# Float16 parts for every fourth group's value products in an attention and feed-forward kernel

## The chip, the cores and the metric

The kernel runs on one core of a Trainium2 chip. The metric is device time in microseconds (us), the median of three runs. The engines are TensorE (PE in the profile; PEld are its weight loads), VectorE (DVE), ScalarE (ACT), GpSimd (POOL) and SyncE (SP), which here issues nearly all DMAs.

## The reference

A transformer block in float32 with a sequence of 2048 rows, width 512, 32 heads of 16 and a hidden width of 1792:

```python
q, k, v = split(layernorm(x) @ wqkv)            # 32 heads of 16
p = softmax(q @ k.T * 16 ** -0.5)               # 2048 x 2048 for each head
h = x + concat(p @ v) @ wo
out = h + silu(layernorm(h) @ w1) @ w2          # w1 512 x 1792, w2 1792 x 512
```

## The kernel before

**Precision.** Most products are made as three float16 products: an operand x is written as a high part (x rounded to float16) and a rest (x minus that, in float16), and high x high, rest x high and high x rest are added in PSUM. `low` (a subtraction on DVE or POOL) makes the rest. The value products, weights p times v, are the exception: they are plain float32 products.

**Stages.** First come the layer norm, the projections and the measuring of the scales of the weights (powers of two). Queries and keys go to DRAM as parts (`qd`, `kd`) and come back for each item: an item is four heads with 512 queries, and there are 32 of them. Rows 0 to 47 of a head's tile hold three parts of 16 rows, and rows 48 to 63 of the query tile are fixed rows: two hold the negative of each query's largest score, the others are zero (`fix_q`). The key tile has a constant (`fix_k`, 2 ** 15) there. One product of 64 rows thus gives the score less its maximum, and the exponential follows without another pass.

**Groups and steps.** An item has 16 groups, a group is 128 keys of its four heads, and 512 steps walk through the groups. Step g makes the score products (`scores`, TensorE), their exponentials (ACT, into `pt` tiles), some searches for maxima of a later item (`maximum`: a product of 48 rows on TensorE and a reduction on DVE), and, at its end, the value products of group g - 2 (`values`, `LAG` is 2). The value products of four heads lie on four strips of 32 columns and add into one PSUM bank, `pv`, over the 16 groups of an item. At the end of an item the bank is copied (`pvs`, on ACT from item 8 on), and the sums and rows go by DMA through DRAM: `sums`, `invert` (POOL) and `spread` follow 2, 6 and 8 steps later, and `divide` (POOL) 10 steps later for every second item.

**The feed-forward part beside attention.** After every 8 items the 512 finished rows go through the output projection (items 8, 16 and 24) and then the feed-forward part. Its products run beside the groups from step 148, 276 and 404 on, 112 steps each: 56 steps of first products (w1) and 56 of second products (w2). There TensorE works on two halves of 64 rows at a time. `beside_products` writes that order by hand: an even step takes the scores of heads 0 and 2 of groups g and g + 1, the odd step after it those of heads 1 and 3 of both, four maxima come in each step, and six half products of the feed-forward part lie beside them. Three PSUM banks are left for scores and three for maxima. A first product ends with a scaling on ACT (`g`), a tanh two steps later and four operations on POOL; a second product takes 14 steps and ends with a scaling on ACT (`g`) and an addition on POOL one step later.

**Order.** Each engine runs its instructions in the order in which the program issues them; helpers pin it. In the profile, lines 99 (products), 102 (transposes), 106 (POOL), 113 (ACT), 123 (DVE) and 129 (DMAs on SP) are those helpers, and 305 and 307 the reductions for maxima.

**Rings.** Keys and queries of an item lie in one of five tiles (`RING`). The weights of the feed-forward part come through eight tiles (`raw_tile`), `pt` has 14 tiles, and `oh` in `zp` two.

Of the kernel before, what the change touches and what calls it, by code (L numbers as in the profile page):

```python
# [10 lines left out]
F32 = mybir.dt.float32  # L11
# [27 lines left out]
LN = 2.0 ** 10  # L39

BOUND = 23.0
PIECES = 14, 14, 4
# [5 lines left out]

LAG = 2
PTS = 14  # L50

RING = 5

HEADS = [(0, 1), (0, 0), (1, 1), (1, 0)]
# [37 lines left out]
def attention_mlp_kernel(ctx: ExitStack, tc: tile.TileContext, x, wqkv, wo, w1, w2, out):  # L92
# [100 lines left out]
    nc.gpsimd.memset(minus, -1.0)  # L193
    ones = const.tile([P, P], F32, name="ones")
    nc.gpsimd.memset(ones, 1.0)
    powers = const.tile([P, 4], F32, name="powers")
    both_s, both_w = powers[:, :2], powers[:, 2:]
    qk_s, qk_w, v_w = (powers[:, n:n + 1] for n in (0, 2, 3))
    qk_e, qk_0, v_f = (const.tile([P, 1], F32, name=name) for name in ("qk_e", "qk_0", "v_f"))

    factors = const.tile([P, 15], F32, name="factors")
    sigma, inverse = factors[:, :4], factors[:, 4:8]
    w1_s, w2_s, wo_s, o_s = (sigma[:, n:n + 1] for n in range(4))
# [47 lines left out]
    va = vpool.tile([P, KC, H, DH + 1], F32, name="va")  # L251

    def rows_of_head(t, h):
        return t[h * DH:(h + 1) * DH].rearrange("d s n -> (d s) n")

    def load_k(i, k, lo=0, n=S):
        a, j = HEADS[k]
        h = 4 * (i % 8) + 2 * a + j
        dma(ks[i % RING][64 * j:64 * j + 48, a, lo:lo + n], rows_of_head(kd, h)[:, lo:lo + n])

    def load_q(i, k):
        a, j = HEADS[k]
        h = 4 * (i % 8) + 2 * a + j
        lo = i // 8 * 512
        dma(qs[i % RING][64 * j:64 * j + 48, a, :], rows_of_head(qd, h)[:, lo:lo + 512])

# [24 lines left out]
    def maximum(i, kb, qt, a, j, n):  # L291

        piece = piece_of(i, a)
        width = 1 if i == LAST else 2
        if piece not in mx:
            mx[piece] = small.tile([P, 64], F32, name="mx", bufs=RING + 1)[:, :32 * width].rearrange(
                "p (j a q k) -> p j a q k", j=2, a=width, k=4)
            left[piece] = 32 * width
        heads = (0, 1) if j is None else (j,)
        for m, h in enumerate(heads):  # L300
            mm(space[:, n + m, :], qs[i % RING][64 * h:64 * h + 48, a, qt * P:qt * P + P],
               ks[i % RING][64 * h:64 * h + 48, a, kb * 512:kb * 512 + 512], start=True, stop=True)
        of = mx[piece][:, :, a % width, qt, kb]
        if j is None:
            pin(nc.vector.tensor_reduce(of, space[:, n:n + 2, :], axis=AX.X, op=ALU.max))  # L305
        else:
            pin(nc.vector.tensor_reduce(of[:, j:j + 1], space[:, n, :], axis=AX.X, op=ALU.max))  # L307
# [42 lines left out]
    def place_far(piece):  # L350

        i, a = piece
        n = 16 if a is None else 8
        mt = small.tile([P, P], F16, name="mt", bufs=1)
        pin(nc.sync.dma_start(mt, wide.pop(piece), transpose=True))
        split.pop(piece)

        def out():
            for j in range(2):
                rows = qs[i % RING][64 * j + 48:64 * j + 50, slice(None) if a is None else slice(a, a + 1)]  # L360
                dma(rows.rearrange("r a n -> r (a n)").rearrange("r (a b) -> r a b", b=P), mt[n * j:n * j + n, :])
            placed.add(piece)

        if at["attention"]:
            soon(1, out)
        else:
            out()

    def place_max(piece):

        i, a = piece
        ns = split.pop(piece)
        n = ns.shape[1]
        ps = bank("sm", F16)
        tr(ps[:n, :P], ns, ident_h)
        mt = small.tile([32, P], F16, name="mn", bufs=1)[:n]
        dve("tensor_copy", mt, ps[:n, :P])

        def out():
            for j in range(2):  # L380
                dst = qs[i % RING][64 * j + 48:64 * j + 50, slice(None) if a is None else slice(a, a + 1)]
# [108 lines left out]


    def pt_tile(name):
        return bp.tile([P, 512], F32, tag="pt", name=name, bufs=PTS)

    def scores(g, k, kind="st"):

        i = g // KC
        a, j, c = head(g, k)
        assert piece_of(i, a) in placed
        ps = bank(kind)  # L500
        mm(ps, ks[i % RING][64 * j:64 * j + 64, a, c * P:(c + 1) * P], qs[i % RING][64 * j:64 * j + 64, a, :],
           start=True, stop=True)
# [39 lines left out]

    rest_sq = const.tile([P, sum(PIECES)], F32, name="rest_sq")
    norms = const.tile([P, 4], F32, name="norms")
# [24 lines left out]
    def set_factors():  # L569
# [4 lines left out]
        for to, a, f in ((h_f, inverse[:, :1], 1 / LN), (g_s, w1_s, 1 / 32.0), (g_half, w1_s, 1 / 64.0),  # L574
                         (out_f, inverse[:, :1], 32.0), (o_minus, o_s, -1.0), (o_twice, o_s, 2.0)):
            pool("tensor_scalar", to, a, f, None, op0=ALU.mult)
        pool("tensor_tensor", out_f, out_f, inverse[:, 1:2], ALU.mult)
        pool("tensor_tensor", wo_f, inverse[:, 2:3], inverse[:, 3:], ALU.mult)
# [27 lines left out]
    def measure(meanwhile):  # L606
# [58 lines left out]
    def project_v(b, t):  # L665
# [3 lines left out]
              {k: (lambda n=n: burst(n)) for k, n in BESIDE_V1.get((b, t), {}).items()})  # L669
        act("mul", va[:, 4 * b + t, :, 0:DH], ps.rearrange("p (h d) -> p h d", d=DH), v_f)  # L670

# [99 lines left out]
    for b in range(NB):  # L771
# [7 lines left out]
        for n, (kind, k) in enumerate(units + vs if b else units):  # L779
# [160 lines left out]
    def finish_part():  # L940
        pvs = bp.tile([P, 512], F32, name="pvs", bufs=1)
        dve("tensor_copy", pvs, pv)
        o_t = zp.tile([P, 4, P], F32, name="o_t", tag="oh")
        pool("memset", o_t, 0.0)
# [4 lines left out]
    def divide_part(part, pvs, o_t, kind="st"):  # L949
# [3 lines left out]
        halves = ps.rearrange("p t (m j r) -> p t m j r", m=2, r=32)[:, :, :, :, :DH + 1]  # L953
        both = gp.tile([P, 4, 2, DH + 1], F32, name="both", bufs=1)
# [110 lines left out]
    def load_rows(b, t):  # L1065
        n = 4 * b + t
        if b < NB - 1:
            hx[t] = raw_tile()
        else:
            hx[t] = ks[(LAST + 1) % RING].rearrange("p a n -> p (a n)").bitcast(F32)[:, t * D:(t + 1) * D]  # L1070
        dma(hx[t], x[n * P:(n + 1) * P, :])
# [89 lines left out]
    def end_first(f, ps):  # L1161
# [3 lines left out]
        def bend():  # L1165
            t = zp.tile([P, 512], F32, name="t", tag="oh")
            act("activation", t, z, AF.Tanh, scale=0.5)
# [262 lines left out]
    def maxima(g):  # L1430

        i, c = divmod(g, KC)
        ready = at["ready"] = min(ITEMS, i + RING - (0 if c == KC - 1 else 1)) * 64
        late_now = at["step"] in late
# [26 lines left out]
    for g in range(groups):  # L1461
# [5 lines left out]
        if (g in beside) != (g - 1 in beside):  # L1467
# [37 lines left out]
        if g == 1:  # L1505
            dve("memset", pv, 0.0)
        at["group"] = g
        n = maxima(g)
# [75 lines left out]
```

## Time and profile before

| | |
|---|---|
| median of three runs | 1543.95 us (1543.88 to 1543.97) |
| the profiled execution | 1544.18 us, its span 1542.3 us |
| busy: TensorE, DVE, ACT, POOL | 1531.9, 1364.3, 1240.0, 575.1 us |
| granted TensorE clock | 1.0 |
| value products | 4096 records (two for each product), 539.1 us |

The profile is one execution. Busy time is the union of an engine's instructions. TensorE's instructions overlap as in a pipeline, so a product's own length (0.38 us for 512 columns of float16) is longer than the distance to the next start. A group's row gives the count, the busy time, the mean length in ns, and the idle time ahead of it with what ended it. In a timeline, rows are start, length, engine, line, operation, names, and a count where several of a kind follow each other.

### The profile page before, as it was taken

To read this page: it belongs to the slowest core of one execution; us is meant where nothing else is said; L and a number is where in the kernel's file an instruction comes from. 1 tells how busy PE (TensorE), PEld (TensorE's weight loads), DVE (VectorE), ACT (ScalarE), POOL (GpSimd) and SP (SyncE) were. 2 spreads that over 40 slices of the span, in tenths; PEclk is the share of its full clock that TensorE was granted. 3 is DMA by queue.
4 is the path that set the end of the run, shared out by engine and by line. 5 is a ranking of instruction groups with operands and counts; after the bars stand their busy time and mean duration, and the time that the engine had idled before them with its cause. 6 is when DMAs were issued, how large, how long until landed. Compare 5 with 4: busy or idle time off the path is not lost.

```text
span 1542.3 us, 30754 instructions
## 1 busy us (share of the span) xinstructions
PE 1531.9 (99%) x11408; PEld 494.6 (32%) x11408; DVE 1364.3 (88%) x2168; ACT 1240.0 (80%) x2410; POOL 575.1 (37%) x782
## 2 busy tenths in 40 slices
PE   9999999999999999999999999999999999999999
PEld 6433322222222333333322333333322333332354
DVE  7899999999999999999999999999999999994322
ACT  5555699999987899888888998888878889888632
POOL 6643453544544444411144444301153444212100
PEclk9999999999999999999999999999999999999999
DMA  6667423333434122245424112444433221335332
GB/s 220 167 170 237 135 80 93 119 96 109 111 89 103 35 63 63 82 147 152 144 64 103 43 46 62 123 131 129 140 81 92 57 56 43 103 103 168 111 91 74
DMA packets 137058, 163.32 MB, mean 106 GB/s; under 512 B 44112, under 2 KB 81040, under 8 KB 136908
## 3 DMA queue, kind: packets, MB, share of 16 engines
q1 hardware_dynamic: 132156, 152.85, 34.6%
q10 hardware_dynamic: 4752, 8.52, 2.1%
q8 instruction: 89, 1.46, 0.4%
q14 instruction: 61, 0.50, 0.1%
HBM read 126.48 MB, written 24.63 MB: 98 GB/s over the span
## 4 chain that ended last, share of the span: by engine, by line
PE 93%; DVE 3%; ACT 2%; issue 1%; POOL 0%; DMA 0%; SPq 0%; POOLq 0%; ACTq 0%
PE ps L99 93%; ACT pt L113 1%; DVE mx L305 1%; DVE mx L307 1%; PE ps L102 1%; DMA ks<-in_A_x_dram 0%; DVE pvs L123 0%; POOL wv_l L106 0%; DVE ks L123 0%; DVE st L123 0%; ACT pvs L113 0%; ACT g L113 0%; DVE ot L123 0%; DVE xtl L123 0%; POOL rs L106 0%
## 5 line engine op out<-in xcount | busy, mean ns | idle before, releaser
L307 DVE TENSOR_REDUCE mx<-ps 128x1 f32<-128x512 f32 x1842 | 1146.1, 682 | 56.2 <-PE ps L99 12.0
L113 ACT ACTIVATE pt<-ps 128x512 f32<-128x512 f32 x2048 | 1049.7, 606 | 130.8 <-PE ps L99 128.7
L99 PE MATMUL ps<-ks,qs 48*128 48x512 f16 x2048 | 666.9, 380 | 2.6 <-DVE mx L307 1.5
L99 PE MATMUL ps<-qs,ks 64*128 64x512 f16 x2048 | 624.8, 377 | 0.6
L99 PE MATMUL ps<-pt,va 128*17 128x512 f32 x4096 | 539.1, 598 | 0.6
L99 PE MATMUL ps<-hts,w 64*128 64x512 f16 (+2 forms) x1212 | 285.0, 372 | 0.0
L99 PEld LDWEIGHTS <-ks 64*128 64x128 f16 x2048 | 174.0, 94 | 223.8 <-issue 177.6
L99 PE MATMUL ps<-w,gates 64*128 64x512 f16 (+1 forms) x938 | 230.3, 378 | 0.2 <-ACT g L113 0.2
L99 PEld LDWEIGHTS <-qs 48*128 48x128 f16 x2048 | 166.4, 94 | 67.7 <-issue 28.4
L99 PEld LDWEIGHTS <-w 64*128 64x128 f16 (+1 forms) x1212 | 101.6, 95 | 236.9 <-ACT pt L113 107.2
L106 POOL TENSOR_TENSOR ri<-rc,minus 128x16 f32<-128x16 f32 x31 | 90.6, 2924 | 208.8 <-DMA rc<-dn 208.8
L99 PEld LDWEIGHTS <-gates 64*128 64x128 f16 (+1 forms) x1082 | 88.7, 95 | 222.5 <-ACT pt L113 97.8
L99 PEld LDWEIGHTS ps<-pt,va 128*17 128x17 f32 x4096 | 68.1, 95 | 195.3 <-issue 186.6
L305 DVE TENSOR_REDUCE mx<-ps 128x2 f32<-128x1024 f32 x103 | 119.1, 1218 | 4.3 <-PE ps L99 3.5
L113 ACT ACTIVATE g<-ps,factors 128x512 f32<-128x512 f32 x80 | 54.7, 684 | 65.1 <-PE ps L99 61.0
L106 POOL TENSOR_SCALAR t<-t,factors 128x512 f32<-128x512 f32 x42 | 29.0, 691 | 184.0 <-ACT t L113 184.0
L113 ACT ACTIVATE ks<-ps 128x512 f32<-128x512 f32 x30 | 17.9, 597 | 51.9 <-PE ps L99 46.6
L106 POOL TENSOR_TENSOR ot<-ot,g 128x512 f32<-128x512 f32 x12 | 15.3, 1271 | 111.6 <-ACT g L113 111.6
L123 DVE SCALAR_TENSOR_TENSOR gh<-g,factors,gh 128x512 f16<-128x512 f32 x14 | 10.5, 752 | 52.1 <-ACT gh L113 52.1
L106 POOL TENSOR_TENSOR t<-t,g 128x512 f32<-128x512 f32 x42 | 53.7, 1279 | 3.5
L106 POOL TENSOR_TENSOR sl<-ks,sh 128x512 f16<-128x512 f32 x30 | 34.7, 1156 | 50.4 <-ACT sh L113 36.9
L106 POOL TENSOR_SCALAR nm<-nm 128x16 f32<-128x16 f32 (+1 forms) x42 | 10.8, 256 | 107.1 <-DVE nm L321 105.5
(158 smaller groups left out, 1029.7 us busy)
## 6 DMA issues: line engine op xcount, KB each, us to landing
w<-w2d SPq DMA_DIRECT2D x182, 256.0 KB
ks<-kd SPq DMA_DIRECT2D x120, 192.0 KB
w<-w1d SPq DMA_DIRECT2D x56, 256.0 KB
ks<-in_B_w_dram ACTq DMA_DIRECT2D x28, 256.0 KB
w<-in_B_w_dram SPq DMA_DIRECT2D x28, 256.0 KB
qs<-qd SPq DMA_DIRECT2D x128, 48.0 KB
kd<-sh SPq DMA_DIRECT2D x16, 256.0 KB
qd<-sh SPq DMA_DIRECT2D x16, 256.0 KB
```

The lines of the kernel that those rows point to most:

```text
L99: return tc.keep_in_program_order(nc.tensor.matmul(*a, **k))
L102: tc.keep_in_program_order(nc.tensor.transpose(*a))
L106: tc.keep_in_program_order(getattr(nc.gpsimd, op)(*a, **k))
L113: ins = getattr(nc.scalar, fn)(*a, **k)
L123: pin(getattr(nc.vector, fn)(*a, **k))
L305: pin(nc.vector.tensor_reduce(of, space[:, n:n + 2, :], axis=AX.X, op=ALU.max))
L307: pin(nc.vector.tensor_reduce(of[:, j:j + 1], space[:, n, :], axis=AX.X, op=ALU.max))
```

## The change

For items 10 to 30, the value products of groups 1, 5, 9 and 13 of an item are made in float16 parts where the group and its neighbours lie beside second products (`in_halves`).
- The exponentials of such a group go to a float32 tile `raw` (from `oh`, now three tiles). The high part is copied to float16 on POOL for heads 0 and 1 and on ACT for heads 2 and 3; the rest is made on POOL. Both lie in the `pt` tile.
- `values` makes twelve float16 products for it: high x high for four heads, high weights x rest of v, rest of weights x high v.
- The parts of v for these four groups of keys are made once, in item 10, on POOL (`split_chunk`). They lie in the fifth tiles of the ring of keys and queries; from item 10 on the ring has four places (`slot`, `loaded`), so an item is loaded three items ahead instead of four. The maxima tiles `mx` go from six to four.
- The fixed rows of the queries hold a constant instead of zeros, made from the scale of queries and keys (`raised`): it raises all weighted scores by 2 ** 14, which drops out in the division by their sum.
- v is kept at another scale: `v_f` and the factor `o_s` go, and the first four chunks of `va` are multiplied by `v_s` on POOL. `ones` and `rest_sq` move to another pool of tiles, `both` to `oh`.

```diff
+RAISE = 14
+MOST = 2.0 ** 15
+HALVED = 1, 5, 9, 13
+FEWER = 2 * RING
...
-    nc.gpsimd.memset(fix_q, 0.0)
+    nc.gpsimd.memset(fix_q, 1.0)
+    raised = const.tile([16, 1], F32, name="raised")
...
+    def slot(i):
+        return i % RING if i < FEWER else (i - FEWER) % (RING - 1)
+    def loaded(i):
+        return min(ITEMS, i + RING if i < FEWER else max(FEWER + RING - 1, i + RING - 1))
...
+    def in_halves(g):
+        i, c = divmod(g, KC)
+        return FEWER <= i < LAST and c in HALVED and all((x - marks[0]) % (8 * KC) in range(BEHIND + 4 * FC, BEHIND + 8 * FC) for x in (g - 1, g + 3))
+    def split_chunk(n):
+        (h, l), v = split_v[n], va[:, HALVED[n]].rearrange("p h d -> p (h d)")
+        pool("tensor_copy", h, v)
+        low(l, v, h, "pool")
...
         def weigh():
             pts[g, k] = pt_tile("pt")
+            if in_halves(g):
+                raw, (h, l) = zp.tile([P, 512], F32, name="raw", tag="oh", bufs=3), halves_of(pts[g, k])
+                ins = act("activation", raw, ps, AF.Exp, scale=qk_f)
+                if k < 2:
+                    pool("tensor_copy", h, raw)
+                else:
+                    act("copy", h, raw)
+                low(l, raw, h, "pool")
+                return ins
             return act("activation", pts[g, k], ps, AF.Exp, scale=qk_f)
...
-        dve("reciprocal", v_f, v_w)
-        pool("tensor_scalar", v_f, v_f, 1 / LN, None, op0=ALU.mult)
...
+        pool("tensor_scalar", raised, qk_s[:16], qk_s[:16], RAISE * math.log(2) / (14 * MX * SCALE), op0=ALU.mult, op1=ALU.mult)
+        pool("tensor_scalar", raised, raised, MOST, None, op0=ALU.min)
+        pool("tensor_scalar", fix_q, fix_q, raised, 1.0, op0=ALU.mult, op1=ALU.mult)
...
+            if b == 2 and 2 <= n:
+                pool("tensor_scalar", va[:, n - 2, :, 0:DH], va[:, n - 2, :, 0:DH], v_s, 1.0, op0=ALU.mult, op1=ALU.mult)
...
     def values(g):
+        if in_halves(g):
+            h_l, v_l = [halves_of(pts.pop((g, k))) for k in range(4)], split_v[HALVED.index(c)]
+            for m, (x, v) in enumerate(((0, 0), (0, 1), (1, 0))):
+                for k in range(4):
+                    a, j, keys = head(g, k)
+                    h = 4 * (i % 8) + 2 * a + j
+                    mm(pv[32 * k:32 * k + DH + 1, :], v_l[v][:, (DH + 1) * h:(DH + 1) * (h + 1)], h_l[k][x],
+                       start=False, stop=m == 2 and c == KC - 1)
+            return
...
-        dve("tensor_scalar", rc, rc, o_s, None, op0=ALU.mult)
...
-        if i + RING - 1 < ITEMS and 6 <= c < 14:
-            (load_k if c % 2 else load_q)(i + RING - 1, c // 2 - 3)
+        if loaded(i) > loaded(i - 1) and 6 <= c < 14:
+            (load_k if c % 2 else load_q)(loaded(i) - 1, c // 2 - 3)
...
+        if i == FEWER and c % 3 == 2 and c < 12:
+            split_chunk(c // 3)
```

More of the change, by code (lines that the diff above doesn't have):

```diff
@@ L193, in attention_mlp_kernel @@
     nc.gpsimd.memset(minus, -1.0)
[L194 to L195 removed]
     powers = const.tile([P, 4], F32, name="powers")
[L197 removed]
+    both_s, both_w, v_s = powers[:, :2], powers[:, 2:], powers[:, 1:2]
     qk_s, qk_w, v_w = (powers[:, n:n + 1] for n in (0, 2, 3))
[L199 removed]
+    qk_e, qk_0 = (const.tile([P, 1], F32, name=name) for name in ("qk_e", "qk_0"))
     factors = const.tile([P, 15], F32, name="factors")
     sigma, inverse = factors[:, :4], factors[:, 4:8]
[L203 removed]
+    w1_s, w2_s, wo_s = (sigma[:, n:n + 1] for n in range(3))
     h_f, g_s, out_f, wo_f, o_minus, o_twice, g_half = (factors[:, n:n + 1] for n in range(8, 15))
     fix_q = const.tile([16, 512], F16, name="fix_q")
[L207 removed]
+    nc.gpsimd.memset(fix_q, 1.0)
+    raised = const.tile([16, 1], F32, name="raised")
     fix_k = const.tile([16, 512], F16, name="fix_k")
@@ L258, in load_k @@
         h = 4 * (i % 8) + 2 * a + j
[L259 removed]
+        dma(ks[slot(i)][64 * j:64 * j + 48, a, lo:lo + n], rows_of_head(kd, h)[:, lo:lo + n])
     def load_q(i, k):
@@ L264, in load_q @@
         lo = i // 8 * 512
-        dma(qs[i % RING][64 * j:64 * j + 48, a, :], rows_of_head(qd, h)[:, lo:lo + 512])
+        dma(qs[slot(i)][64 * j:64 * j + 48, a, :], rows_of_head(qd, h)[:, lo:lo + 512])
     def fixed_rows(i):
@@ L295, in maximum @@
         if piece not in mx:
-            mx[piece] = small.tile([P, 64], F32, name="mx", bufs=RING + 1)[:, :32 * width].rearrange(
+            mx[piece] = small.tile([P, 64], F32, name="mx", bufs=RING - 1)[:, :32 * width].rearrange(
                 "p (j a q k) -> p j a q k", j=2, a=width, k=4)
@@ L300, in maximum @@
         for m, h in enumerate(heads):
-            mm(space[:, n + m, :], qs[i % RING][64 * h:64 * h + 48, a, qt * P:qt * P + P],
-               ks[i % RING][64 * h:64 * h + 48, a, kb * 512:kb * 512 + 512], start=True, stop=True)
+            mm(space[:, n + m, :], qs[slot(i)][64 * h:64 * h + 48, a, qt * P:qt * P + P],
+               ks[slot(i)][64 * h:64 * h + 48, a, kb * 512:kb * 512 + 512], start=True, stop=True)
         of = mx[piece][:, :, a % width, qt, kb]
@@ L359, in out @@
             for j in range(2):
-                rows = qs[i % RING][64 * j + 48:64 * j + 50, slice(None) if a is None else slice(a, a + 1)]
+                rows = qs[slot(i)][64 * j + 48:64 * j + 50, slice(None) if a is None else slice(a, a + 1)]
                 dma(rows.rearrange("r a n -> r (a n)").rearrange("r (a b) -> r a b", b=P), mt[n * j:n * j + n, :])
@@ L380, in out @@
             for j in range(2):
-                dst = qs[i % RING][64 * j + 48:64 * j + 50, slice(None) if a is None else slice(a, a + 1)]
+                dst = qs[slot(i)][64 * j + 48:64 * j + 50, slice(None) if a is None else slice(a, a + 1)]
                 dst = dst.rearrange("r a n -> r (a n)").rearrange("r (a b) -> r a b", b=P)
@@ L489, in attention_mlp_kernel, with halves_of @@
     free = [sum(x not in fixed for x in range(g)) for g in range(groups + 1)]
+    def halves_of(t):
+        return t.bitcast(F16)[:, :512], t.bitcast(F16)[:, 512:]
+    width = H * (DH + 1)
+    spare_k, spare_q = (t.rearrange("p a n -> p (a n)") for t in (ks[RING - 1], qs[RING - 1]))
+    parts = [spare_k[:, n * width:(n + 1) * width] for n in range(7)] + [spare_q[:, :width]]
+    split_v = [(parts[n], parts[4 + n]) for n in range(4)]
     def pt_tile(name):
         return bp.tile([P, 512], F32, tag="pt", name=name, bufs=PTS)
+    def in_halves(g):
[5 more added lines that the diff above has]
+        low(l, v, h, "pool")
     def scores(g, k, kind="st"):
@@ L541, in attention_mlp_kernel @@
     sq = small.tile([P, 3], F32, name="sq", bufs=1)
-    rest_sq = const.tile([P, sum(PIECES)], F32, name="rest_sq")
+    rest_sq = wp.tile([P, sum(PIECES)], F32, name="rest_sq")
+    ones = wp.tile([P, P], F32, name="ones")
+    nc.gpsimd.memset(ones, 1.0)
     norms = const.tile([P, 4], F32, name="norms")
@@ L942, in finish_part @@
         dve("tensor_copy", pvs, pv)
-        o_t = zp.tile([P, 4, P], F32, name="o_t", tag="oh")
+        o_t = zp.tile([P, 4, P], F32, name="o_t", tag="oh", bufs=3)
         pool("memset", o_t, 0.0)
@@ L1165, in bend @@
         def bend():
-            t = zp.tile([P, 512], F32, name="t", tag="oh")
+            t = zp.tile([P, 512], F32, name="t", tag="oh", bufs=3)
             act("activation", t, z, AF.Tanh, scale=0.5)
@@ L1432, in maxima @@
         i, c = divmod(g, KC)
-        ready = at["ready"] = min(ITEMS, i + RING - (0 if c == KC - 1 else 1)) * 64
+        ready = at["ready"] = loaded(i if c == KC - 1 else i - 1) * 64
         late_now = at["step"] in late
```

12 lines of the change are left out of this document (7 added, 5 removed).

## The prediction

> **What bounds the kernel now.** First I read the page: the busy times, the chain that ended last, the costliest groups.
>
> ```profile
> span 1542.3 us, 30754 instructions
> ...
> PE 1531.9 (99%) x11408; PEld 494.6 (32%) x11408; DVE 1364.3 (88%) x2168; ACT 1240.0 (80%) x2410; POOL 575.1 (37%) x782
> ...
> PE ps L99 93%; ACT pt L113 1%; DVE mx L305 1%; DVE mx L307 1%; PE ps L102 1%; DMA ks<-in_A_x_dram 0%; DVE pvs L123 0%; POOL wv_l L106 0%; DVE ks L123 0%; DVE st L123 0%; ACT pvs L113 0%; ACT g L113 0%; DVE ot L123 0%; DVE xtl L123 0%; POOL rs L106 0%
> ...
> L99 PE MATMUL ps<-pt,va 128*17 128x512 f32 x4096 | 539.1, 598 | 0.6
> ```
>
> TensorE is the bound: 99% busy, 93% of the chain. The value products are 4096 records, two for each float32 product, so 512 groups of four heads. Next, the stretches that the change touches: busy time by engine (PE, PEld, DVE, ACT, POOL) in the second products, and the chain in the first of them.
>
> ```profile
> 641.00:770.00 129.00, 129.00 (x1088) 41.76 (x1088) 122.99 (x202) 105.69 (x205) 20.56 (x28) 1.00 0.47 142
> 976.00:1109.00 133.00, 133.00 (x1124) 43.02 (x1122) 126.84 (x208) 109.25 (x211) 24.00 (x34) 1.00 0.46 135
> 1317.00:1380.00 63.00, 63.00 (x534) 20.39 (x529) 60.14 (x100) 52.09 (x102) 10.31 (x17) 1.00 0.32 98
> ...
> 640.97 129.21 PE ps L99 x1085
> ```
>
> TensorE has no gap here, its clock is 1.00, and the chain is TensorE alone. ACT has 18% idle, POOL 84%, DVE 5%. A shorter value product is thus worth its whole saving, as long as ACT and DVE keep up.
>
> **The gain.** One step of that stretch, in order of time on TensorE (start, length):
>
> ```profile
> 700.03 0.39 PE L99 MATMUL ps<-w,gates 64*128 64x512 f16 x1
> ...
> 701.12 0.38 PE L99 MATMUL ps<-w,gates 64*128 64x512 f16 x1
> ...
> 701.33 0.38 PE L99 MATMUL ps<-ks,qs 48*128 48x512 f16 x1
> 701.35 0.37 PE L99 MATMUL ps<-qs,ks 64*128 64x512 f16 x1
> 701.65 0.62 PE L99 MATMUL ps<-pt,va 128*17 128x512 f32 x4
> ...
> 702.10 0.61 PE L99 MATMUL ps<-pt,va 128*17 128x512 f32 x4
> ...
> 702.64 0.39 PE L99 MATMUL ps<-w,gates 64*128 64x512 f16 x1
> 702.87 0.38 PE L99 MATMUL ps<-w,gates 64*128 64x512 f16 x1
> ```
>
> A step lasts 2.61 us (700.03 to 702.64). The four heads' products run side by side on four column strips: the first halves start at 701.65, the second at 702.10, the next product of another shape at 702.64: 0.45 + 0.54 = 0.99 us. A float16 product of 512 columns takes 0.21 us to the next start (701.12 to 701.33), 0.23 just after a change of shape (702.64 to 702.87); a float32 half is two such passes. Three rounds of float16: 0.23 + 0.23 + (0.54 - 0.21) = 0.79, so 0.20 us is saved in each split group. How four float16 strips follow each other no row shows; the bounds are 0.09 us more per round, if the third round's weights aren't loaded ahead, and 0.78 for the three at the plain spacing. I take 0.20.
>
> The condition in `in_halves` asks for items 10 to 30, every fourth group (1, 5, 9, 13 of 16), and neighbours in the second products, which are groups 204 to 259, 332 to 387 and 460 on. That leaves 205 to 253, 333 to 381 and 461 to 493: 13 + 13 + 9 = 35 groups. 35 x 0.20 = **7.0 us gained**.
>
> **What ACT pays.** Of a split group, heads 0 and 2 get their exponentials at the end of the even step, 1 and 3 at the end of the odd one. The last of each (2 and 3) is followed on ACT by a copy to float16. Rows of ACT: a step with nothing added, one with the copy of the value sums (`pvs`), one with a product's scaling (`g`), and the nearest row to the new copy.
>
> ```profile
> 690.25 2.06 ACT L113 ACTIVATE pt<-ps 128x512 f32<-128x512 f32 x4 [0.55 <-PE ps L99]
> 692.32 0.58 ACT L113 COPY pvs<-ps 128x512 f32<-128x512 f32 x1
> 692.84 0.60 ACT L113 ACTIVATE pt<-ps 128x512 f32<-128x512 f32 x1
> ...
> 669.32 1.10 ACT L113 ACTIVATE pt<-ps 128x512 f32<-128x512 f32 x2 [0.54 <-PE ps L99]
> 670.31 0.68 ACT L113 ACTIVATE g<-ps,factors 128x512 f32<-128x512 f32 x1
> 670.88 2.14 ACT L113 ACTIVATE pt<-ps 128x512 f32<-128x512 f32 x4
> ...
> 175.50 0.60 ACT L113 ACTIVATE ks<-ps 128x512 f32<-128x512 f32 x1 [0.17 <-PE ps L99]
> 176.13 0.62 ACT L113 CAST sh<-ks 128x512 f16<-128x512 f32 x1
> 176.65 0.59 ACT L113 ACTIVATE pt<-ps 128x512 f32<-128x512 f32 x1
> ```
>
> Four exponentials take 2.06 us, and ACT then idles 0.55 us for the next step's first score. A copy of what ACT has just written starts 0.03 us after the write's end (175.50 + 0.60, 176.13) and holds the next instruction up by 0.52 (176.13 to 176.65): 0.55 in all. It just fits the gap. The `pvs` copy alone (0.52) and `g` alone (0.57) fit it too. Two of them don't: ACT is then about 0.52 to 0.57 us late. What lateness costs is shown by four rows of another stretch, where ACT's first exponential of a step came late:
>
> ```profile
> 832.17 2.06 ACT L113 ACTIVATE pt<-ps 128x512 f32<-128x512 f32 x4 [0.58 <-PE ps L99]
> ...
> 832.77 0.38 PE L99 MATMUL ps<-ks,qs 48*128 48x512 f16 x1
> 832.82 0.37 PE L99 MATMUL ps<-qs,ks 64*128 64x512 f16 x1
> 833.12 1.05 PE L99 MATMUL ps<-pt,va 128*17 128x512 f32 x8
> ...
> 700.67 1.59 ACT L113 ACTIVATE pt<-ps 128x512 f32<-128x512 f32 x3 [0.54 <-PE ps L99]
> ```
>
> Three score banks are left in these steps, so the fourth score waits for the first exponential: it starts 0.05 us after that one's end (832.17 + 0.60, 832.82), and the value products stand behind it. In a normal step the first exponential ends at 701.27 and the fourth score starts at 701.35: 0.08, so 0.03 us of slack. A late ACT thus costs TensorE its lateness less 0.03, once; the shifted step then gives ACT its gap back.
> - Copies in a step with nothing else: lateness 0.00 to 0.03, cost 0 each; if the cover is gone, 70 x 0.01 and up (a rival below).
> - Group 1 of an item: its odd step also has the `pvs` copy of the item before. These are 209, 225, 241, 337, 353, 369, 465, 481: 8 x (0.52 - 0.03) = **3.9 us lost**.
> - A second product ends every 14 steps, at 217, 231, 245, 345, 359, 373, 473, 487; 217, 245, 345, 373 and 473 are split steps, where `g` meets the copy: 5 x (0.57 - 0.03) = **2.7 us lost**.
>
> **What POOL pays.** Two copies and four subtractions per split group; nearest rows, then what already runs there.
>
> ```profile
> L106 POOL TENSOR_TENSOR gates<-t,gates 128x512 f16<-128x512 f32 x42 | 48.6, 1158 | 3.4
> ...
> L106 POOL CAST gates<-t 128x512 f16<-128x512 f32 x42 | 25.6, 610 | 2.7
> ...
> 700.01 2.92 POOL L106 TENSOR_TENSOR ri<-rc,minus 128x16 f32<-128x16 f32 x1 [21.93 <-DMA rc<-dn]
> ...
> 703.78 0.22 POOL L106 TENSOR_TENSOR ri<-ri,rc 128x16 f32<-128x16 f32 x1
> 707.65 1.27 POOL L106 TENSOR_TENSOR ot<-ot,g 128x512 f32<-128x512 f32 x1 [3.65 <-ACT g L113]
> ```
>
> 2 x 0.61 + 4 x 1.16 = 5.9 us in each 10.4 us. From the even step's start: third exponential ends at 0.64 + 2 x 0.49 + 0.60 = 2.2, copy to 2.9, remainders to 4.2 and 5.4; in the odd step copy to 6.1, remainders to 7.3 and 8.5. The value products need them at 3 x 2.61 + 1.6 = 9.4: 0.9 us of slack. The fourth raw tile takes the first one's place in a ring of three, freed at 4.2, wanted at 2.61 + 2.1 = 4.7. From 8.5 to the next copy at 12.7 POOL is free. The reciprocal of the sums (700.01 to 704.00, 4.0 us), which POOL's order now puts behind the remainders, fits: 12.5. What is queued behind it is its store to DRAM on SP, 5 us later than now, and the weight loads behind that one; the sums' DMA chain is next needed four steps on, and I cost it at nothing (bounds 0 and 2 us). At 232, 360 and 488 the store of finished rows (1.27) comes in between too: the next copy is 1.1 late, the ring's free slot 0.6, ACT 0.6: 3 x 0.57, the last partly covered by the longer steps near the end: **1.4 us lost**.
>
> **The rest together.** DVE needs 4 x 0.61 us per step (122.99 us for 202 instructions) = 2.44, against 2.41 in the short step and 2.61 in the three beside it: 0. Four scalings of `va`, three small operations for `raised` and eight operations for the values' parts lie on POOL where it waits (0, bounds -0.2 and +1). With four instead of five places in the ring, an item's keys are loaded three items ahead, not four; their maxima begin four steps before the item ahead of it does, so 0. The reciprocal `v_f` and the factor in `divide_part` go: 0 to -0.2. For these and for copies that just miss I put +0.3.
>
> **Sum:** -7.0 + 3.9 + 2.7 + 1.4 + 0.3 = +1.3. The profiled execution took 1544.18 us (span 1542.3 and 1.9 around it), so 1545.5; the median is 0.23 lower, which gives 1545.2. A measurement tells this kernel from no change at about 0.2%, 3.1 us, so this is no change.
>
> **Rivals.**
> 1. *The pile-ups don't reach TensorE* (faster). If ACT takes the copy earlier or shorter, or the fourth score has more slack than 0.03, the 8.3 us fall away and the gain stands: 1544 - 7 = 1537. For it: TensorE never stalls now with one extra operation per gap. Against: two of 0.52 in 0.55. Half of the pile-ups gone gives 1541. Chance of ending below 1540.9: 0.27.
> 2. *Each copy misses the gap* (slower). Place: the last exponential of a step, the copy, the next step's first. It decides from 0.58 us on; at 0.70 each of 70 copies costs 0.12: +8.4, 1553. For it: the fit has nothing to spare. Against: the `sh` row. Chance 0.11.
> 3. *TensorE can't be fed twelve products in 0.79 us* (slower). Now eight records take 0.99, 0.12 each, and 14 between 700.03 and 701.65 take 0.116 each; no row shows 0.065. At half the saving: 1545.2 + 3.5 = 1548.7. Against: the four starts of a round lie 0.02 us apart together (0.62 against 0.60 for one), so a stock of them stands ready. Chance 0.07. The Trainium skill, "TensorE: Matmul & The Clock Gate", section "Wait — 56ns, not 53.3ns?", speaks for this rival: with hardware decode off, the sequencer spends about 62 ns on each matmul. By that figure an estimate for the group is 12 x 62 ns = 0.74 and its drain, which leaves some 0.1 of the saving; no row here shows which decoding this chip uses.
> 4. *POOL in its order waits for a DMA* (the sums or the denominators) with the copies behind it: 1 to 2 us at each of 8 items, some 1553. Against: POOL's free 4.2 us in every four steps take up as much. Chance 0.05.
>
> **How the numbers follow.** Mine, within 1540.9 to 1547.0: 0.50. Faster 0.27 (rival 1), slower 0.23 (rivals 2 to 4). The likeliest case's own range is 1541 to 1547; the range that leaves out 2 in 10 reaches from the whole gain, 1537.2, to rival 3 with a part of 2, 1550.
>
> **What would show it.** Split groups: twelve records of 128*17 float16 in 0.79 us, third round 0.23 behind the second. Steps 210, 226, 242 near 3.1 us instead of 2.61, with the fourth score late and ACT without idle time; 218 and 246 too. Split steps' values at 2.41. If 210 and 218 stay at 2.61, my losses are wrong; if all even steps grow, rival 2; if rounds take 0.30, rival 3.

## The result, and the profile after

The changed kernel takes 1552.89 us (median of four runs, 1552.43 to 1553.5) against 1543.93 us of the kernel before beside it: ratio 1.0058, interval 1.0041 to 1.0076. It is slower by 9.0 us, where 1545.2 was predicted and 1550 was the upper end.

The profiled execution took 1552.43 us. Its page gives the busy times and the chain that ended last:

```profile
span 1550.6 us, 31348 instructions
...
PE 1534.4 (99%) x11548; PEld 498.1 (32%) x11548; DVE 1362.8 (88%) x2165; ACT 1275.1 (82%) x2480; POOL 785.5 (51%) x1006
...
PE 82%; ACT 6%; DVE 5%; POOL 3%; issue 1%; DMA 1%; SPq 0%; POOLq 0%; DVEq 0%; ACTq 0%
```

The chain was TensorE's to 93% before, with 2% for ScalarE and 0% for GpSimd. Now it is TensorE's to 82%; 6% of it is ScalarE's and 3% GpSimd's. (In this kernel the helpers' lines are 108 for products, 115 POOL, 122 ACT, 132 DVE, 138 DMAs; 322 and 336 are reductions for maxima.) The busy times of the first stretch of second products, columns as before:

```profile
641.00:770.00 129.00, 127.12 (x1116) 42.02 (x1116) 120.05 (x198) 116.15 (x225) 91.18 (x103) 1.00 0.46 135
```

TensorE had no gap there; it now lacks 1.88 us of busy time, its clock still 1.00. POOL went from 20.56 to 91.18 us. But busy time shows little of the loss: two pipelined products overlap (0.38 us long, 0.21 us apart), so a late start shows as a gap only when it is longer than a product's tail.

The better measure is the start of each group's value products, in the two traces. Interval 205, say, is the time from the start of group 205's to that of group 206's; since a step makes the products of the group two before it, it is step 208. Outside the three stretches the intervals differ by 0.1 us or less in sum; within them they differ at a few places only (after less before, us):

| intervals | each | sum |
|---|---|---|
| 202, 330, 458 (and 0.03 at the next): a stretch's start, fourth score late | +0.52 | +1.56 |
| 205, 333, 461: a stretch's start, its first split group, saving already taken off | +1.47 | +4.41 |
| eight behind the odd step of a group 1 (207, 223 ... 479) | +0.49 | +3.9 |
| 215, 243, 343, 371, 471: `g` meets a copy | +0.55 | +2.8 |
| 492: the scores of group 493 made in one step | +1.30 | +1.3 |
| 231, 359 (and 0.03 at 499) | +0.08 | +0.2 |
| 21 split groups with their whole saving | -0.23 | -4.8 |
| 229, 357, 485 half; 481 nearly nothing | -0.11 | -0.4 |
| 217, 233, 249, 345, 361, 377, 473: nothing | 0.00 | 0 |

The sum is 9.0, and the medians lie 9.0 apart. (The two traces themselves lie 8.3 apart: the changed one starts its first value products 0.24 earlier and has a tail 0.34 shorter, for which no cause is shown.) Three things in it stand nowhere in the prediction: the starts of the stretches, interval 492, and the groups that gain nothing.

**A split group that goes as planned.** TensorE's timeline of the changed kernel, one in the stretch (the twelve as one row) and one near the end (round by round). The parts of v lie in tiles of the ring of keys and queries, so their names are `ks` and `qs`:

```profile
656.76 0.83 PE L108 MATMUL ps<-pt,ks 128*17 128x512 f16 x12
657.52 0.39 PE L108 MATMUL ps<-ks,qs 48*128 48x512 f16 x1
...
1418.11 0.39 PE L108 MATMUL ps<-pt,ks 128*17 128x512 f16 x4
1418.33 0.39 PE L108 MATMUL ps<-pt,qs 128*17 128x512 f16 x4
1418.55 0.39 PE L108 MATMUL ps<-pt,ks 128*17 128x512 f16 x4
1418.87 0.61 PE L108 MATMUL ps<-qs,ks 64*128 64x512 f16 x4
```

The rounds start 0.22, 0.22 and, to the next shape, 0.32 us apart: 0.76 us for the twelve (656.76 to 657.52) where the eight records took 0.99. That saves 0.23.

**The start of a stretch.** The chain of waits of the changed kernel around group 205 (start, length, what):

```profile
636.65 0.61 POOL pt L115
...
637.34 2.27 POOL pt L115 x2
639.61 0.69 POOL t L115
...
640.37 1.28 POOL t L115
...
641.70 0.62 POOL gates L115
...
642.39 1.16 POOL gates L115
643.55 0.55 POOL pt L115
...
644.18 2.28 POOL pt L115 x2
```

and TensorE's timeline there:

```profile
638.29 0.38 PE L108 MATMUL ps<-ks,qs 48*128 48x512 f16 x1
638.79 0.37 PE L108 MATMUL ps<-qs,ks 64*128 64x512 f16 x1
...
644.35 0.40 PE L108 MATMUL ps<-pt,ks 128*17 128x512 f16 x4
...
644.79 0.38 PE L108 MATMUL ps<-pt,ks 128*17 128x512 f16 x1
645.39 0.39 PE L108 MATMUL ps<-pt,ks 128*17 128x512 f16 x2 [0.23 <-POOL pt L115]
646.50 0.38 PE L108 MATMUL ps<-pt,ks 128*17 128x512 f16 x1 [0.72 <-POOL pt L115]
```

The last first product's tanh comes due two steps after its scaling, in the first steps of the second products. It lies in ACT's gap together with the copy for head 2: the fourth score starts 0.50 after the third (638.29 to 638.79) instead of 0.02. Its four operations on POOL (`t`, `t`, `gates`, `gates`, 639.61 to 643.55) stand in POOL's order between the copy and the rests for heads 0 and 2 and those for heads 1 and 3. So the last rests are made at 646.46, and the third round of group 205, which should follow at 644.79, ends its starts at 646.50. Interval 205 is 4.08 us, 1.70 longer than a short one.

**ScalarE's pile-up**, behind the odd step of a group 1 (interval 207), ACT's and TensorE's timelines:

```profile
651.07 1.09 ACT L122 ACTIVATE raw<-ps 128x512 f32<-128x512 f32 x2
652.19 0.62 ACT L122 CAST pt<-raw 128x512 f16<-128x512 f32 x1
652.72 0.58 ACT L122 COPY pvs<-ps 128x512 f32<-128x512 f32 x1
653.19 2.06 ACT L122 ACTIVATE pt<-ps 128x512 f32<-128x512 f32 x4
```

```profile
653.34 0.38 PE L108 MATMUL ps<-ks,qs 48*128 48x512 f16 x1
653.85 0.37 PE L108 MATMUL ps<-qs,ks 64*128 64x512 f16 x1
```

ACT has no idle time, and the fourth score starts 0.51 behind the third: the prediction's pile-up, at its size. The interval is 3.10 us.

**Interval 492.** By then no maxima are left, and a step takes all four scores of one group. ACT's timeline:

```profile
1410.74 1.57 ACT L122 ACTIVATE raw<-ps 128x512 f32<-128x512 f32 x3 [0.42 <-PE ps L108]
...
1414.07 0.60 ACT L122 ACTIVATE raw<-ps 128x512 f32<-128x512 f32 x1 [1.10 <-POOL pt L115]
```

Four `raw` tiles are wanted in one step from a ring of three. The fourth waits 1.10 us for POOL to finish with the first, and the next scores wait behind it. The ring is not all of it: POOL's copy and first rest took 1.03 and 1.53 us here, 0.8 us more together than elsewhere (rows in the last section). At their usual lengths some 0.3 of the 1.10 us would be left, an estimate.

### The profile page after: what moved, and what is told of

Same layout as the page of the kernel before. It is cut to its first block, busy times and chain, and to the rows that moved or that the text cites. A ratio compares the mean times of both kernels' runs of the same rounds, so it can differ in the third digit from the quotient of the medians.

```text
span 1550.6 us, 31348 instructions
## 1 busy us (share of the span) xinstructions
PE 1534.4 (99%) x11548; PEld 498.1 (32%) x11548; DVE 1362.8 (88%) x2165; ACT 1275.1 (82%) x2480; POOL 785.5 (51%) x1006
## 3 DMA queue, kind: packets, MB, share of 16 engines
q8 instruction: 90, 1.47, 0.4%
## 4 chain that ended last, share of the span: by engine, by line
PE 82%; ACT 6%; DVE 5%; POOL 3%; issue 1%; DMA 1%; SPq 0%; POOLq 0%; DVEq 0%; ACTq 0%
PE ps L108 82%; ACT pt L122 4%; DVE mx L322 2%; POOL pt L115 1%; DVE mx L320 1%; ACT raw L122 1%; POOL ri L115 1%; ACT pvs L122 0%; PE ps L111 0%; POOL t L115 0%; DMA ks<-in_A_x_dram 0%; DMA va<-in_A_wqkv_dram 0%; POOL gates L115 0%; DVE st L132 0%; DVE pvs L132 0%
## 5 line engine op out<-in xcount | busy, mean ns | idle before, releaser
L122 ACT ACTIVATE pt<-ps 128x512 f32<-128x512 f32 x1908 | 979.1, 607 | 100.1 <-PE ps L108 96.9
L108 PE MATMUL ps<-pt,va 128*17 128x512 f32 x3816 | 502.2, 598 | 0.6
L108 PEld LDWEIGHTS <-ks 64*128 64x128 f16 (+1 forms) x2424 | 181.8, 93 | 243.8 <-issue 194.2
L115 POOL TENSOR_TENSOR pt<-raw,pt 128x512 f16<-128x512 f32 x140 | 159.7, 1162 | 5.6
L108 PEld LDWEIGHTS ps<-pt,va 128*17 128x17 f32 x3816 | 63.4, 95 | 192.1 <-issue 183.3
L115 POOL CAST pt<-raw 128x512 f16<-128x512 f32 x70 | 43.1, 615 | 75.0 <-ACT raw L122 75.0
L122 ACT ACTIVATE raw<-ps 128x512 f32<-128x512 f32 x140 | 76.7, 608 | 1.5 <-POOL pt L115 1.1
```

The lines of the kernel that those rows point to most:

```text
L108: return tc.keep_in_program_order(nc.tensor.matmul(*a, **k))
L115: tc.keep_in_program_order(getattr(nc.gpsimd, op)(*a, **k))
L122: ins = getattr(nc.scalar, fn)(*a, **k)
```

## The experiments

Each is the changed kernel with the edit shown, timed beside the kernel before on the same chip (1543.85 to 1544.2 us there).

**The rest alone.** No group is split; the ring of four, the raise, the scalings and the parts of v stay.

```diff
-        return FEWER <= i < LAST and c in HALVED and all(
+        return False and FEWER <= i < LAST and c in HALVED and all(
```

> The changed kernel with no group in float16 parts: value products all float32 as before; the rest of the change (fixed rows, four places in the ring, scalings, the parts of v in item 10) stays. Theory (the loss is made in the stretches with split groups: 2.2 us at each of three starts, pile-ups on ACT, one stall of 1.3 us at the end): value products start 0.3 us earlier than before up to step 203 already, so 1543.6 us. Rival (the ring, the layout of the tiles or the other edits cost time): above 1545.

1543.96 us, ratio 0.9999 (0.9989 to 1.0009). All that surrounds the split groups costs nothing that can be measured.

**The products alone.** The exponential writes the high part directly; no copies, no low parts of the weights.

```diff
-                raw, (h, l) = zp.tile(...), halves_of(pts[g, k])
...
-                low(l, raw, h, "pool")
-                return ins
+                return act("activation", halves_of(pts[g, k])[0], ps, AF.Exp, scale=qk_f)
...
-                    mm(..., h_l[k][x],
+                    mm(..., h_l[k][0],
```

> The 35 groups make their twelve float16 products, but no copies and no remainders: the exponential is written straight to the high part and the third round reads that again, so the remainders of the weights are left out. Theory (TensorE's saving is real, 0.23 us per group, and is lost to ACT and POOL; the 7 groups 9 lose it to DVE): 1543.6 - 28 x 0.23 = 1537.2 us. Rival (three rounds of float16 don't pay here): 1543 or more.

1538.3 us, ratio 0.9962 (0.9948 to 0.9976). The saving is real and reaches the end: 5.9 us. So the loss of the change, 14.6 us above this, comes from the copies and rests. The same groups as in the changed kernel gain half or nothing, although ACT and POOL have nothing to do for them here. For 229 the timelines of this kernel show why (ACT's first, then TensorE's):

```profile
704.78 1.10 ACT L122 ACTIVATE pt<-ps 128x512 f32<-128x512 f32 x2 [0.54 <-PE ps L108]
705.77 0.68 ACT L122 ACTIVATE g<-ps,factors 128x512 f32<-128x512 f32 x1
706.34 3.04 ACT L122 ACTIVATE pt<-ps 128x512 f32<-128x512 f32 x6
```

```profile
707.82 0.38 PE L108 MATMUL ps<-ks,qs 48*128 48x512 f16 x1
707.97 0.37 PE L108 MATMUL ps<-qs,ks 64*128 64x512 f16 x1
```

`g` and four exponentials need 0.57 + 4 x 0.49 = 2.53 us of ACT, more than the short step's 2.38; the fourth score is 0.13 late. So it is ACT, and not POOL, that holds 229 and 357.

**The first split group of each stretch left as it was.**

```diff
-            ... for x in (g - 1, g + 3))
+            ... for x in (g - 3, g + 3))
```

> The changed kernel without the first split group of each stretch (205, 333, 461 stay float32). Theory (there the last first product's tanh and its four POOL operations stand between the group's copies; 0.5 us on ACT and 1.7 us of waiting products, each time): 1552.9 - 3 x (2.2 - 0.23) = 1547.0 us. Rival (each split group loses a little, by copies that miss the gap on ACT): 32 of 35 parts of the loss stay, 1552.1.

1547.59 us, ratio 1.0022 (1.0012 to 1.0032). Three groups of 35 cost 5.3 us.

**The last tanh two steps later**, behind that group's copies, the groups all split.

```diff
-        soon(2, bend)
+        soon(4 if f == FC - 1 and at["next"] > FEWER * KC else 2, bend)
```

> The changed kernel with all 35 groups, but the tanh and the four POOL operations of the last first product of a stretch come four steps after its end instead of two, behind the first split group's copies. Theory: the three starts lose nothing, 1552.9 - 3 x 2.2 = 1546.3 us. Rival (the start is slow for another reason, such as DMAs or the ring of raw tiles): 1552 to 1553.

1546.36 us, ratio 1.0014 (1.0005 to 1.0024): 6.5 us back, with only the order changed. The operations themselves cost nothing; where they stood in two queues did.

**Only the POOL operations of that tanh one step later**, the tanh where it was.

```diff
-            pool("tensor_scalar", t, t, 1.0, g_half, ...)
...
+            def on_pool():
+                pool("tensor_scalar", t, t, 1.0, g_half, ...)
...
+            if f < FC - 1:
+                on_pool()
+            else:
+                soon(1, on_pool)
```

> All 35 groups; only the four POOL operations of each last first product come one step later, behind the copies of the first split group; its tanh on ACT stays where the change has it. Theory (of 2.2 us at a start, 1.7 are POOL's order and 0.5 ACT's pile-up of tanh and copy): 1552.9 - 3 x 1.7 = 1547.8 us. Rival (ACT alone makes the start slow): 1552.9. Rival (POOL alone): 1546.4, as with the tanh moved too.

1548.25 us, ratio 1.0027 (1.0016 to 1.0037): 4.6 us of the 6.5. So the stall at a stretch's start is to some 70% POOL's order and otherwise ACT's crowded gap.

**Head 3's copy on POOL where ACT would be crowded** (groups 1, and those that meet `g`).

```diff
-                if k < 2:
+                if k < 2 or k == 3 and (c == 1 or ends_second(g)):
```

> All 35 groups, but in the 13 where ACT has a second extra operation in the gap after the odd step (the copy of the value sums in the 8 groups 1, the scaling of a finished second product in 217, 245, 345, 373, 473), the copy of head 3 is made on POOL instead of ACT. Theory (two extra operations miss the gap of 0.55 us and stall the fourth score by 0.5): 1552.9 - 13 x 0.5 = 1546.4 us. Rival (the stall comes from elsewhere in these steps): 1552.9, or more where POOL's 0.6 us lets products wait.

1549.49 us, ratio 1.0036 (1.0023 to 1.0048), 3.1 us above the expectation. The 13 late scores are gone: intervals 207 and 215 last 2.61 again. But at two places, ahead of groups 249 and 377, POOL's longer queue met the addition of `g` and the reciprocal of the sums. POOL's and ACT's timelines:

```profile
748.55 1.28 POOL L115 TENSOR_TENSOR ot<-ot,g 128x512 f32<-128x512 f32 x1
749.77 2.94 POOL L115 TENSOR_TENSOR ri<-rc,minus 128x16 f32<-128x16 f32 x1
...
753.72 0.61 POOL L115 CAST pt<-raw 128x512 f16<-128x512 f32 x1
```

```profile
755.60 0.60 ACT L122 ACTIVATE raw<-ps 128x512 f32<-128x512 f32 x1 [1.06 <-POOL pt L115]
```

That cost 1.15 us each time (intervals 247 and 375). In the profiled execution a score also waited once, 1.14 us, for the DMA of the queries' fixed rows (`qs<-mt`):

```profile
1031.53 0.37 PE L108 MATMUL ps<-qs,ks 64*128 64x512 f16 x1 [1.14 <-DMA qs<-mt]
```

A copy moved off one engine was paid for where the other had its own pile-up.

**No groups 9** (but for 489, which gains).

```diff
-        return ... and c in HALVED and all(
+        return ... and c in HALVED and (c != 9 or g == 489) and all(
```

> The changed kernel without its groups 9 of an item, save 489 (7 groups go back to float32: 217, 233, 249, 345, 361, 377, 473). Theory (what they save on TensorE is taken by DVE, which in the step after the short one has a reduction for the next item's maxima of 0.22 us besides its four): the saving of 7 x 0.23 was never there, and the three pile-ups of 217, 345 and 473 go: 1552.9 - 3 x 0.55 = 1551.2 us. Rival (groups 9 gain like the others): 1551.2 + 1.6 = 1552.8.

1551.53 us, ratio 1.0048 (1.0032 to 1.0065). That is 1.4 us below the change, about the spread of its four runs, so the trace has to tell. Those groups gain nothing and still cost something: three of the five meetings of `g` with a copy (215, 343, 471) are theirs, and are gone.

**Without group 493.**

```diff
+        ... and g != 493
```

> The change without its last group, 493, which lies where all four scores of a group come in one step; its products stay float32 and its weighted scores are not raised. In the changed kernel the value products after group 493 lose 1.30 us, of which 0.23 would be given back by the three products. Theory (the fourth raw tile of that step waits for GpSimd's copy, since one step needs four tiles of a ring of three): 1552.9 - 1.1 = 1551.8 us. Rival (the loss there is taken up by the tail, which is the same in both kernels): 1552.9 us.

1552.17 us, ratio 1.0053 (1.0036 to 1.007), between the theory and its rival, and its own distance to the change is within the spread of the runs. The trace tells both apart. In interval 492 the 1.30 us are gone, and with them 0.23 of saving; in interval 499 the program waits for weights that came no earlier, and gives 0.69 back:

```profile
1435.18 0.38 PE L108 MATMUL ps<-w,gates 128*128 128x512 f16 x1 [0.56 <-DMA w<-w2d]
```

So the wait for the raw tile was there, and half of it had covered a later wait for a DMA. The run takes away POOL's longer operations together with the fourth tile, so it does not separate the two. (The raise of the weighted scores stays for all groups; the edit changes only how 493's products are made.)

**The repairs together**: the late tanh, head 3's copy on POOL as above, no groups 9 but 489, no 493; 27 groups are split.

> All mendings in one: the last first product's tanh and POOL operations two steps later, the copy of head 3 on POOL in groups 1 and where a second product ends, no groups 9 but 489, and no 493 (whose four scores come in one step, so that its fourth raw tile waits 1.1 us for the ring of three). 27 groups are left. Theory: 1543.9 - 27 x 0.23 = 1537.7, and up to 1539 with what the two groups 229 and 357 lose to POOL. Rival (the losses move elsewhere): 1544 or more.

1538.48 us, ratio 0.9963 (0.9949 to 0.9977): faster than both kernels. From its page:

```profile
PE 1525.7 (99%) x11516; PEld 496.4 (32%) x11516; DVE 1363.1 (89%) x2165; ACT 1261.4 (82%) x2454; POOL 747.1 (49%) x968
...
PE 92%; DVE 5%; ACT 2%; issue 1%; DMA 0%; POOL 0%; SPq 0%; POOLq 0%; DVEq 0%; ACTq 0%
```

POOL does nearly as much as in the change (747.1 against 785.5 us) and is out of the chain. For these 27 groups neither engine has too much work; what had cost time was the place of some operations in the order and, for ten copies, the engine that made them.

**Why groups 9 gain nothing.** In the step behind their shorter products VectorE reduces an item's maxima to one per query, 0.22 us. Two runs were to move it to POOL, in the kernel with the products alone and in the kernel with the repairs ("the best one" below) with all groups 9 taken in again.

The edit beside those of the two kernels (the last condition, cut here, asks for the second products):

```diff
-            finish_max(piece, g is not None and g > FIRSTS[0] * KC)
+            finish_max(piece, ... and not (g // KC < LAST and g % KC == 12 and ...))
```

> The kernel with the products alone (no copies, no low parts; the low parts are left out, two of the three products use the high part), and in it the 0.22 us reduction to the negated maximum of step 12 in the stretches of second products is given to GpSimd in place of VectorE. Theory (the groups 9 gain nothing because VectorE has that reduction between two maxima in the step behind the shortened one): the seven groups gain their 0.23 us as the others do, 1538.3 - 7 x 0.23 = 1536.7 us. Rival (something else of that step holds them, the store of g or the order of the scores): 1538.3 us, unchanged.

> The version with the late bend, with head 3's copy on GpSimd where two of ScalarE's copies would crowd and without group 493, with the groups 9 taken in again and the negated maximum of step 12 on GpSimd in the stretches of second products. Theory (VectorE's reduction alone held the groups 9 back, and GpSimd has room): 1538.5 - 7 x 0.23 = 1536.9 us. Rival (the reduction is longer on GpSimd and comes between its subtractions, so that a later copy or a raw tile waits): 1538.5 us or more.

1538.16 us (0.9962, 0.9948 to 0.9976) and 1541.85 us (0.9986, 0.9977 to 0.9996). The condition named the wrong step (12 for 11), so it moved nothing (in both traces VectorE still makes all 24 of these reductions): the first is the products alone once more, 0.14 from the earlier time; the second is the best one with groups 9, which cost it 3.4 us: in its trace 1.15 each ahead of 249 and 377 as above, and 1.43 in interval 499, in a wait for weights (`w<-w2d`). With the right step, in the kernel with the products alone:

> The kernel with the products alone, in which the reduction to the negated maximum is really taken off VectorE in the stretches of second products: the last attempt named step 12, while the kernel places that reduction in step 11, so nothing was moved. GpSimd now finds the maximum of four in six small operations; the low parts are left out as before. Theory (VectorE's 0.22 us between two maxima in the step of a group 9 holds it back): the seven groups gain 0.23 us each as the others do, 1538.2 - 1.6 = 1536.6 us. Rival (something else of that step holds them): 1538.2 us.

1536.78 us, ratio 0.9952 (0.9935 to 0.9968). All seven groups now gain their 0.23 us; 0.48 of the 1.6 goes back in interval 499. VectorE's timelines, of the products alone and of this kernel:

```profile
673.69 2.48 DVE L322 TENSOR_REDUCE mx<-ps 128x1 f32<-128x512 f32 x4
676.28 0.22 DVE L336 TENSOR_REDUCE nm<-mx 128x16 f32<-128x64 f32 x1
676.42 3.19 DVE L322 TENSOR_REDUCE mx<-ps 128x1 f32<-128x512 f32 x5
```

```profile
673.48 5.69 DVE L322 TENSOR_REDUCE mx<-ps 128x1 f32<-128x512 f32 x9
```

VectorE has no idle time in either. In the first the step's last product for a maximum (48 rows) starts 0.43 behind the score ahead of it, 676.72 to 677.15, where 0.20 is usual; its bank is still being read:

```profile
676.72 0.38 PE L108 MATMUL ps<-qs,ks 64*128 64x512 f16 x1
677.15 0.37 PE L108 MATMUL ps<-ks,qs 48*128 48x512 f16 x1
```

This settles the groups 9. Then the reduction was moved in the kernel with the repairs too, with the groups 9 taken in but for 249 and 377:

> The version with the late bend, head 3's copy on GpSimd where ScalarE would be crowded, and without group 493, with the reduction moved to GpSimd and the groups 9 taken in but for 249 and 377, whose copies stand behind the store of g and cost 1.15 us each. Theory (VectorE's reduction holds the five others back, and GpSimd's six operations fit between its subtractions): 1538.5 - 5 x 0.23 = 1537.3 us. Rival (the six operations push copies back, or the reduction isn't what holds them): 1538.5 us or more.

1541.7 us, ratio 0.9985 (0.9975 to 0.9994), the rival. Interval 217 is 2.38 us, so VectorE is free; but POOL's six small operations lie ahead of the copies, and a raw tile waits two steps on. POOL's and ACT's timelines:

```profile
675.85 0.24 POOL L115 TENSOR_TENSOR mx<-mx 128x32 f32<-128x32 f32 x1 [0.50 <-DVE mx L322]
...
677.54 0.23 POOL L115 TENSOR_TENSOR nm<-nm,mx 128x16 f32<-128x16 f32 x1
...
678.62 0.61 POOL L115 CAST pt<-raw 128x512 f16<-128x512 f32 x1
```

```profile
680.50 0.60 ACT L122 ACTIVATE raw<-ps 128x512 f32<-128x512 f32 x1 [0.44 <-POOL pt L115]
```

Interval 219 is 0.54 longer than in the kernel with the repairs, and it is 0.54 to 0.62 at each of the four other places. Another 0.28 each is lost behind 249 and 377, where the reduction is on POOL too, and 0.9 in interval 349, 0.52 of it again a wait for `qs<-mt`. Of the kernels that make all parts, the one with the repairs and without groups 9 stays the best.

## Why the prediction was wrong

- **The saving: right.** 0.20 was taken for a group, 0.23 measured; the twelve products take 0.76 us, not 0.79. Rival 3 falls. The Trainium skill's page "TensorE: Matmul & The Clock Gate", section "Wait — 56ns, not 53.3ns?", gives some 62 ns for a matmul with hardware decode off, an estimate of 0.74 us for the twelve. The trace does not show that pace: rounds of four start 0.22 us apart, 0.055 for each product. The 0.76 are two such distances and the 0.32 to the next shape, so the saving was not cut to the 0.1 that the prediction read from that figure.
- **The count of 35: wrong by 2.2 us.** 21 groups got the whole saving and the three first ones theirs within a loss. The step that failed here is "DVE needs 4 x 0.61 us per step = 2.44, against 2.41 in the short step ...: 0". It left out the 0.22 us reduction, which falls into the short step of seven groups (1.6 us; shown by the run that moved it). And `g` on ACT was counted where it meets a copy, not where it falls into a short step (0.12 each at 229 and 357; seen in the timeline of the products alone). Groups 481 and 485, 0.3 us together, show the same two things there, though no run tests them: such a reduction (0.19 us at 1373.78) lies in the step behind 481, whose last product for a maximum starts 0.40 behind the score ahead of it, and a `g` (at 1382.79) in the step behind 485.
- **ACT's pile-ups: right.** 0.49 at eight places was predicted and measured; at the five ends of second products 0.55 against 0.54. Rival 1 falls with it. Steps 210, 226 and so on (intervals 207, 223) have the 3.10 us written there.
- **Quiet copies cost nothing: right.** Rival 2 put a price on each of the 70 copies and came to 1553, close to the time; but the losses stand at few places, and the intervals with other copies are 2.61 or 2.38. The time alone would have spoken for a rival that the trace refutes.
- **POOL's part: wrong, and the greatest term, at the starts of the stretches.** "From 8.5 to the next copy at 12.7 POOL is free" was worked out for a cycle in the middle of a stretch, from rows at 700 us. The first cycle still holds the last first product's tanh and its four POOL operations. That is 2.0 us of net loss in each of three stretches, 6.0 in all, where the prediction has nothing; the late tanh gave 6.5 back. Some 1.5 of the 2.0 are POOL's order. The other 0.5 is ACT's: "What ACT pays" counted the `pvs` copy and `g` as what a copy can meet, and left out this tanh. Rival 4 had the mechanism, POOL's order, with the wrong thing in front: at none of the places in the table does a copy stand behind a wait for a DMA.
- **Additions of `g` on POOL at 232, 360 and 488: over-sized.** 1.4 us predicted, 0.15 measured at the two first, nothing at the third. Ahead of 233 the copy was 0.7 us late (712.98 instead of 0.67 behind the start of its exponential at 711.61), and the slack of the ring took nearly all of it.
- **The last group: missed.** The prediction used the order of `beside_products` for all split groups. Group 493 lies where a step takes four scores of one group, so a ring of three is short by one, and POOL's longer operations there add to it: 1.3 us.
- **The rest: right.** No difference beyond the noise of 1.5 us, where +0.3 was put.

Together: -7.0 became -5.2 outside the stretch starts, the pile-ups were +6.7, the POOL term of 1.4 became 0.2, and 6.0 and 1.3 came on top: 9.0.

## What to carry to other kernels

Work that fits into a steady cycle must also fit into the first cycle after a change of mode and into the last: walk through those by hand, with what the mode before still has queued on each engine, since on an engine that runs in order a copy waits for every operation in front of it. Before counting a saving for each of n places, list for every engine the rare small operations that fall into some of them: here a reduction of 0.22 us took the whole saving of 0.23 at seven places. And when a forecast of loss comes out near the time, look whether it stands at the places that it named.

## What was not expected of the hardware

The twelve float16 products on four column strips take 0.76 us, 0.063 each; rounds of four start 0.22 apart, 0.055 for each product. The densest stretch shown of before has 0.116. Near the end, beside group 493, two of POOL's operations were longer than the same ones elsewhere. POOL's and VectorE's timelines:

```profile
1411.40 1.03 POOL L115 CAST pt<-raw 128x512 f16<-128x512 f32 x1 [2.06 <-ACT raw L122]
1412.51 1.53 POOL L115 TENSOR_TENSOR pt<-raw,pt 128x512 f16<-128x512 f32 x1
1413.98 0.61 POOL L115 CAST pt<-raw 128x512 f16<-128x512 f32 x1
```

```profile
1411.88 0.55 DVE L132 CAST hts<-ot 128x384 f16<-128x384 f32 x1
1412.46 0.56 DVE L132 TENSOR_TENSOR hts<-ot,hts 128x384 f16<-128x384 f32 x1
```

0.61 and 1.14 are usual in the stretch (636.65, and half of the pair at 637.34). These two are the only ones of their kind that run beside VectorE's splitting of the finished rows (`hts`), which ends at 1413.02; the next copy, at 1413.98, has its usual length again. The five traces of other edits that split group 493 with copies and rests show the same: 1.02 to 1.03 and 1.52 to 1.53 us at this place, and at most 0.62 and 1.18 at every other. So the two go together; no run moves VectorE's operations away to prove that they are the cause.
